# Attention in exact fp32 for all batches, and partition maxima on TensorE, in an attention and two-layer mixture-of-experts kernel

## The chip, the cores and the metric

The kernel runs on one core of a Trainium2 chip. A core has TensorE (in the profile PE for products, PEld for weight loads), VectorE (DVE), ScalarE (ACT), GpSimd (POOL) and SyncE (SP, which here starts the DMA transfers of inputs). The metric is the device time of one execution in microseconds; lower is better.

## The reference

Sparse attention of 4 batches, 8 heads, 576 positions and 64 dimensions; four heads see a local window of 32 positions, four every 32nd position. Its output is the input of a mixture of 8 experts with Sinkhorn-balanced gate, and that one's output the input of a second mixture, whose tokens are assigned greedily by sorted logits.

```python
def _attn_ref(q, k, v):
    scores = scale * np.matmul(q, k.transpose(0, 1, 3, 2))
    mask_local = (rel >= 0) & (rel < 32)
    mask_strided = (rel >= 0) & (pos[None, :] % 32 == pos[:, None] % 32)
    ...
    scores = scores - np.max(scores, axis=-1, keepdims=True)
    attn = np.exp(scores)
    attn = attn / (np.sum(attn, axis=-1, keepdims=True) + 1e-09)
    return np.matmul(attn, v)

def _moe_ref(x, w_gate, w1, w2):          # x: 2304 x 512
    P = np.exp(x @ w_gate - max)          # then 8 times: rows, columns to sum 1, times N / E
    for e in range(8):
        out += P[:, e:e + 1] * (np.maximum(x @ w1[e], 0.0) @ w2[e])

def _moe2_ref(x, w_gate, w1, w2):         # each token to one expert, 288 to each
    ...
```

## The kernel before

Large products are made in f16 with a split of each operand into a high and a low half: high by high, high by low and low by high, three f16 products in place of one fp32 product. Weights and inputs are scaled by a power of two, which needs the absolute maximum of the whole tensor, so a maximum over partitions: `att_scale` for V of each batch, `w_scale` for expert weights, `gate_w` for the gate. VectorE reduces along the columns, and `partition_all_reduce` on GpSimd over the 128 partitions (lines 194, 485, 546).

The attention works in units: batch, kind of mask (local with 6 groups of 96 queries by 128 keys; strided with 8 groups of 72 by 72) and pair of heads, 16 units, four to a batch. Within a unit the two heads lie on partitions 0 to 63 and 64 to 127 of q and k. The steps of a unit are load (L), halves of q and k (K, `att_k`, line 235), scores (S0, S1, `att_s`), mask and maximum (M), exponentials (E), row sums, reciprocal and normalising (N, the multiply on GpSimd, line 325), transposes of the probabilities by a product with the identity (T), and output products with V (O), whose result is split into the high and low half of x (`split_out`, lines 232 and 233). M, E, N and T are made for each head (0 or 1) by itself, O for each half of the groups.

Batch 0 (`EXACT`) is in plain fp32: one product per group and head, the mask added on TensorE by a bf16 product with the identity, the maximum read from PSUM, exponentials with the maximum as bias. Batches 1 to 3 use halves: q, k, the probabilities and V are split (V in `att_v`), the mask is added on VectorE (294), the maximum subtracted on GpSimd (297). While batch 0 is worked on, `busy` (158) puts extra bf16 products on TensorE, whose results are not used.

In the same stage run, by one string of letters (`SEQ`, line 47), the preparation of expert 0's weights (W for w1, V for w2: four column maxima, the scale, eight splits of 512 columns each), V of batch 1 (E), the load of w2 (R), the gate (G, H), constants (C), and Q: the first six jobs of 256 tokens of expert 0, as three pairs of jobs. A pair is 32 units: 16 groups of 12 products in layer 1 (`l1`, 614, with high half on ACT 617, low half on DVE 618) and 16 quarters of 24 products in layer 2 (`l2`, 632). A pair needs x of its tokens, so pair 1 batch 0, pair 2 batch 1, pair 3 batch 2. Each letter issues the next step of its generator; every engine works through its own instructions in the order in which they are issued, and waits where an operand or a buffer isn't ready. After the last letter the gate of the last five blocks of tokens (`gate(13, NT)`) ends the stage.

PSUM has eight banks: four with the tag "bank" (scores, transposes, outputs) and four "l1" (expert 0, gate, and batch 0's second kind of use).

The rest of the kernel, from the softmax of the gate on, is left as it is: expert 0's other jobs and experts 1 to 7, the second gate, the assignment, the second mixture.

Of the kernel before, what the change touches and what calls it, by code (L numbers as in the profile page):

```python
# [51 lines left out]
SPAD = 2  # L52
# [49 lines left out]
class Kernel:  # L102
# [11 lines left out]
    def abank(self, u, name):  # L114

        return self.bank(name, "l1" if u[0] == 0 and u[2] == 0 else "bank")
# [15 lines left out]

    def att_consts(self, pool):
# [3 lines left out]
        self.mk, self.mb = [], []  # L137
        for kind in range(2):
            P, G, W = self.GEO[kind]
            m = self.acc[:P, 16 + kind, 0:4 * W].rearrange("p (g w) -> p g w", w=W)  # L140
            nc.sync.dma_start(out=m, in_=self.a[f"mask{kind}"])
            self.mk.append(m)
# [5 lines left out]
        self.att_v_tiles(pool)  # L148

    GEO = (96, 6, 128), (72, 8, 72)  # L150
    GROUPS = ((0, 4), (4, 6)), ((0, 4), (4, 8))
    KQ = WIN + 2 * S
# [7 lines left out]
    def att_load_v(self, b, parts=None):  # L160

        nc = self.nc
        if not parts:
            parts = []
            for n, p, g in (("vl", 128, 6), ("vs", 72, 8)):
                t = self.ald.tile([p, 4, g, D], F32, name=n, bufs=1)
                nc.sync.dma_start(out=t, in_=self.a[n][b])
                parts.append((t[:, 0:2], t[:, 2:4]))
        else:
            for ts, n in zip(parts, ("vl", "vs")):  # L170
                for hp, t in enumerate(ts):
                    nc.sync.dma_start(out=t, in_=self.a[n][b, :, 2 * hp:2 * hp + 2])
        self.avr[b] = parts
# [7 lines left out]
    def att_scale(self, b):  # L181
# [3 lines left out]
        mx = sm.tile([128, 8], F32, name="vmx")  # L185
        nc.gpsimd.memset(mx, 0.0)
        for kind, p in enumerate((128, 72)):
            for hp, t in enumerate(self.avr[b][kind]):
                k = 2 * kind + hp
                nc.vector.tensor_reduce(mx[0:p, k:k + 1], t, axis=AX.XYZ, op=OP.max, apply_absolute_value=True)  # L190
                yield
        nc.vector.tensor_reduce(mx[:, 0:1], mx, axis=AX.X, op=OP.max)
# [16 lines left out]
    def att_v_tiles(self, pool):  # L209

        self.av = []
        for kind, (p, g) in enumerate(((128, 6), (72, 8))):
            ts = [pool.tile([p, 2, g, 192], F16, name=f"v{x}{kind}") for x in "ho"]
            for t in ts:
                self.nc.gpsimd.memset(t[:, :, :, D:2 * D], 0.0)
            self.av.append(ts)
# [256 lines left out]
    def w_scale(self, r, j, inv, early):  # L473
# [12 lines left out]
        if early:  # L486
            yield
# [999 lines left out]
```

## Time and profile before

| | |
|---|---|
| median of 3 runs | 2003.76 us (2003.56 to 2011.95) |
| the profiled execution | 2007.91 us |
| its span, first to last instruction | 2006.2 us, mean granted clock 0.969 |
| TensorE products, busy | 1889.4 us, 94% of the span |
| VectorE, ScalarE, GpSimd, busy | 1146.1, 526.4, 227.4 us |
| first product of expert 0 (line 614) | 81.45 us |
| last gate product of the stage (line 566) | ends at 306.64 us |

Times are those of one profiled execution. A busy TensorE is not one at its peak: products are pipelined, so in a dense row the time from start to start is the price, not the length. The granted clock is a share of full speed (2.4 GHz); 0.5 is the lower of its two levels, 1.2 GHz. A wait is put down to what came last before it ended.

### The profile page before, as it was taken

The numbers are of one execution on the slowest core, as the hardware profiler recorded it, in microseconds if no ns is written. First come the engines' busy times: TensorE is split into PE (matmuls) and PEld (weight loads), VectorE is DVE, ScalarE is ACT, GpSimd is POOL, SyncE is SP. The second block draws the span as 40 slices with busy tenths as digits, with TensorE's granted clock in tenths as the row PEclk, the third lists the DMA queues.
The fourth block names the chain that finished last, engine by engine and source line by source line (L and its number), as shares of the span: only waits on it lengthen the run. The fifth ranks groups of instructions, "written<-read, shape, count | busy, mean of one in ns | idle before, by whom it ended". The sixth has DMA issues, their size and how long they took to land. (4 is left out here: it accounts for less than half of the span.)

```text
span 2006.2 us, 29660 instructions
## 1 busy us (share of the span) xinstructions
PE 1889.4 (94%) x12406; PEld 1051.3 (52%) x12406; DVE 1146.1 (57%) x2779; ACT 526.4 (26%) x944; POOL 227.4 (11%) x250
## 2 busy tenths in 40 slices
PE   5579899999999999999999999999999999989997
PEld 3457576444544454445445444545454444666676
DVE  5677667465536554665455465434854788665530
ACT  3355343132122222111122123121201110232343
POOL 2426430000000000000000000000000003132231
PEclk7689999999999999999999999999999999999999
DMA  5302002114422431211134214321100003344360
GB/s 179 116 13 77 19 7 86 42 46 146 145 84 84 168 121 56 76 43 43 42 126 168 84 69 150 118 84 43 42 1 11 22 22 124 112 171 144 117 216 25
DMA packets 54302, 172.65 MB, mean 86 GB/s; under 512 B 4736, under 2 KB 9416, under 8 KB 49728
## 3 DMA queue, kind: packets, MB, share of 16 engines
q1 hardware_dynamic: 46488, 127.75, 18.0%
q0 software_dynamic: 7680, 43.01, 6.0%
q8 instruction: 97, 1.59, 0.3%
q14 instruction: 37, 0.30, 0.1%
HBM read 127.20 MB, written 43.54 MB: 85 GB/s over the span
## 5 line engine op out<-in xcount | busy, mean ns | idle before, releaser
L614 PE MATMUL l<-xh,w1h 128*128 128x512 f16 (+1 forms) x1408 | 482.8, 343 | 20.8 <-DVE hl L618 19.7
L614 PE MATMUL l<-xl,w1h 128*128 128x512 f16 (+1 forms) x1408 | 482.9, 343 | 0.0
L614 PE MATMUL l<-xh,w1l 128*128 128x512 f16 (+1 forms) x1408 | 482.6, 343 | 0.0
L632 PE MATMUL l<-w2h,hh 128*128 128x512 f16 x1152 | 438.3, 380 | 0.0
L632 PE MATMUL l<-w2h,hl 128*128 128x512 f16 x1152 | 438.0, 380 | 0.0
L632 PE MATMUL l<-w2l,hh 128*128 128x512 f16 x1152 | 437.9, 380 | 0.0
L614 PEld LDWEIGHTS <-w1h 128*128 128x128 f16 x2816 | 276.9, 99 | 249.6 <-issue 23.8
L617 ACT ACTIVATE hh<-l 128x512 f16<-128x512 f32 (+1 forms) x352 | 180.9, 517 | 767.5 <-PE l L614 767.1
L632 PEld LDWEIGHTS <-hh 128*128 128x128 f16 x2304 | 222.7, 98 | 260.4 <-issue 4.3
L618 DVE SCALAR_TENSOR_TENSOR hl<-l,hh 128x512 f16<-128x512 f32 (+1 forms) x352 | 206.2, 589 | 224.8 <-ACT hh L617 224.5
L664 DVE SCALAR_TENSOR_TENSOR acc<-l,pe,acc 128x512 f32<-128x512 f32 x126 | 94.2, 747 | 193.2 <-PE l L632 192.9
L614 PEld LDWEIGHTS <-w1l 128*128 128x128 f16 x1408 | 139.1, 99 | 112.9
L632 PEld LDWEIGHTS <-hl 128*128 128x128 f16 x1152 | 112.9, 98 | 136.8 <-issue 1.6
L479 DVE TENSOR_REDUCE wmx<-raw 128x1 f32<-128x1024 f32 x120 | 141.2, 1209 | 68.3 <-DMA raw<-in_moe_w_dram 68.3
L485 POOL PARTITION_ALL_REDUCE wall<-wmx x32 | 11.3, 352 | 974.5 <-DVE wmx L483 962.6
L498 ACT ACTIVATE m2h<-raw,wscale 128x1024 f16<-128x1024 f32 x64 | 70.4, 1140 | 192.1 <-DVE iw L492 89.0
L499 DVE SCALAR_TENSOR_TENSOR m2l<-raw,wscale,m2h 128x1024 f16<-128x1024 f32 x64 | 80.1, 1281 | 49.7 <-DMA wd<-m2l 28.4
L789 DVE SCALAR_TENSOR_TENSOR junk<-acc,raw 128x512 f32<-128x512 f32 x144 | 98.9, 687 | 3.3 <-DMA raw<-gt 1.4
L1258 DVE TENSOR_TENSOR h2l<-h,h2h 128x288 f16<-128x288 f32 x64 | 28.9, 454 | 65.4 <-ACT h2h L1257 58.2
L824 DVE SCALAR_TENSOR_TENSOR junk<-raw 128x256 f32<-128x256 f32 x128 | 54.1, 423 | 11.1 <-DMA raw<-in_moe_w_dram 7.6
L498 ACT ACTIVATE w2h<-raw,wscale 128x1024 f16<-128x1024 f32 x28 | 30.1, 1137 | 94.8 <-DVE wscale L129 94.8
L325 POOL TENSOR_TENSOR sm<-sm,den 96x768 f32<-96x768 f32 (+1 forms) x32 | 43.0, 1345 | 89.9 <-DVE den L323 26.5
(342 smaller groups left out, 1892.1 us busy)
## 6 DMA issues: line engine op xcount, KB each, us to landing
raw<-in_moe_w_dram SPq DMA_DIRECT2D x30, 2048.0 KB, 9.2
wd<-m2h SPq DMA_DIRECT2D x32, 512.0 KB, 2.6
wd<-m2l SPq DMA_DIRECT2D x32, 512.0 KB, 3.1
kq<-in_qk_dram SPq DMA_DIRECT2D x16, 592.0 KB, 3.8
acc<-in_moe_w_dram SPq DMA_DIRECT2D x2, 2048.0 KB, 10.9
vl<-in_vl_dram SPq DMA_DIRECT2D x3, 768.0 KB
raw<-gt SPq DMA_DIRECT2D x2, 1024.0 KB, 6.3
raw<-in_moe_w_dram SPq DMA_DIRECT2D x2, 1024.0 KB, 8.7
```

Of the source, the lines that this page charges most:

```text
L325: e.tensor_tensor(sm, sm, den[:, :, None].to_broadcast([P, G, W]), op=OP.mult)
L479: nc.vector.tensor_reduce(mx[:, k:k + 1], r[:, k * n:k * n + n], axis=AX.XY, op=OP.max, apply_absolute_value=True)
L498: nc.scalar.activation(hi, raw, AF.Copy, scale=s)
L499: nc.vector.scalar_tensor_tensor(lo, raw, s, hi, op0=OP.mult, op1=OP.subtract)
L614: nc.tensor.matmul(ps, l[:, d, fs], r[:, d, t0:t0 + nb], start=k == 0, stop=k == 3 * DC - 1)
L617: self.last = [nc.scalar.activation(hh[:, f, :nb], ps, AF.Relu).ins, nc.vector.scalar_tensor_tensor(hl[:, f, :nb], ps, 0.0, hh[:, f, :nb], ...
L618: nc.vector.scalar_tensor_tensor(hl[:, f, :nb], ps, 0.0, hh[:, f, :nb], op0=OP.max, op1=OP.subtract).ins]
L632: nc.tensor.matmul(ps, l[:, f, js], r[:, f], start=k == 0, stop=k == 3 * FC - 1)
L664: self.last = [nc.vector.scalar_tensor_tensor(a, ps, pe[:, c:c + 1], a, op0=OP.mult, op1=OP.add).ins]
L789: self.nc.vector.scalar_tensor_tensor(junk, self.acc[:, c], 1.0, self.wgb[:, e], op0=OP.mult, op1=OP.mult, accum_out=self.lg[:, c, e:e + 1])
L824: nc.vector.scalar_tensor_tensor(junk[:, :n], w[:, c], 1.0, g[:, e], op0=OP.mult, op1=OP.mult, accum_out=part[:, i, c, e:e + 1])
L1258: nc.vector.tensor_tensor(hl[:, f], r, hh[:, f], op=OP.subtract)
```

## The change

All four batches take the fp32 path. The step is now a piece: half the groups of a unit (3 of the local kind, 4 of the strided), both heads together in one instruction where an instruction can hold them, 32 pieces. The halves of q, k, probabilities and V go (`att_k`, `att_v`, `att_early`, `att_side`), and so do the mask on VectorE and the subtraction on GpSimd. Output products (O) and their split into x (X) are steps of their own. Scores have a pair of banks "s" (batch 0 alternates with "t"), transposes from batch 1 on a pair "t", outputs one bank "o", everything else three banks "l1".

The maxima over partitions in this stage (V of each batch, the gate's weights, both weights of expert 0) are made by `all_max`: a product with the identity brings the columns to rows, VectorE reduces them and puts the results on a diagonal, a product with ones spreads them to all partitions, and VectorE reduces again. The other experts' weights stay with GpSimd. w2's splits of expert 0 all go by ACT and DVE (`WM`), `busy` is called with 3, 5 and 1 products rather than 2 each, masks get buffers of their own, V has two buffers, and `SEQ` puts four Q to each piece from batch 1 on (`UNIT`).

```diff
--- before
+++ after
-EXACT = (0,)
-BUSY = 2, 2, 2, 2
+BUSY = 3, 5, 1
 START = 20
 PAD = 4
-PSCALE = 1024.0
 KQ_BUFS, SM_BUFS, P_BUFS = 3, 3, 2
-NORM = ("pp", "pp", "pp", "pp")
-PRO = "V V V V M0 M1", "E0", "N0", "E1", "N1 V V"
-FIRST = [("L K S0 S1", "M0", "E0", "T0", "T1", "M1", "E1", "N0", "O0", "N1", "O1")] * 4
-NEXT = "L K S0 S1 M0", "T0 M1", "T1", "E0 N0", "O0", "E1 N1", "O1"
-SIDE = 4
+PRO = "S0 M0", "S1 M1", "E0", "N0"
+FIRST = "S2 M2", "O-1", "E1", "X-1", "T0", "N1"
+TURN = "S1 M1", "O-1", "E1", "X-1", "T0", "N1"
+NEXT = "S1 M1", "O-1", "E1", "X-1", "T0", "N1"
+UNIT = "AQAAQAQQAA"
+SEQ = ("A" * 12 + "AWAWAWAW" + "R" + "A" * 4 + "WAWAWA" + "AWAWAWAWAWAWAWAW" + "A" * 11 + "AVAAVAAVAAVAAAAA" + "VAQVAAVQVAQVQAAV" + "VAQAAVQVAQVQAAV" + "VVU" + "UUUUUAAA" +
+       "G" + "U" * 8 + "AAHC" + "U" * 8 + "AA").replace("U", UNIT) + "Q" * 20
+WM = "aaaaaaaa"
+SPAD = 0
 NW = 8
-UNIT = "AQQAQAQAQAQAQAQ"
-UNIT = "AQQAQAQAQAQAQAQ"
-LESS = "AQQAQAAQAAQA"
-UNIT = "AQQAQAQAQAQAQAQ"
-LESS = "AQQAQAAQAAQA"
-SEQ = ("A" * 12 + "AWAWAWAW" + "R" + "A" * 6 + "W" + "AWAWAWAWAWAWAWAWAWAW" + "A" * 10 + "AVAVAVAV" + "AAAEE" + "A" + "EQ" * 4 + "VEQ" * 2 + "A" + "VEQVEQ" + "AEVQAVQ" + "EVQEVQ" + "EVQ" + "EVEVQA" + "AEVQLLL" +
-       "GUUUUHCUUUU").replace("U", UNIT).replace("L", LESS) + "Q" * 20
-WM = "aaaapapa"
-EPAD = 1
-VPAD = 0
-SPAD = 2
...
+    def all_max(self, cols, out):
+        nc = self.nc
+        k = cols.shape[1]
+        yield
+        ps = self.bank("amx", "l1")
+        nc.tensor.matmul(ps[:k, 0:128], cols, self.identf, start=True, stop=True)
+        m = self.asm.tile([4, 1], F32, name="amax")[:k]
+        nc.vector.tensor_reduce(m, ps[:k, 0:128], axis=AX.X, op=OP.max)
+        d = self.asm.tile([4, 4], F32, name="adiag")[:k, :k]
+        nc.vector.tensor_scalar(d, self.identf[:k, :k], m, None, op0=OP.mult)
+        yield
+        yield
+        nc.tensor.matmul(ps[:, 128:128 + k], self.onesf[:k], d, start=True, stop=True)
+        nc.vector.tensor_reduce(out, ps[:, 128:128 + k], axis=AX.X, op=OP.max)
...
+    GROUPS = ((0, 3), (3, 6)), ((0, 4), (4, 8))
-    GROUPS = ((0, 4), (4, 6)), ((0, 4), (4, 8))
...
-        nc.gpsimd.partition_all_reduce(al, mx[:, 0:1], channels=128, reduce_op=bass_isa.ReduceOp.max)
-        yield
+        yield from self.all_max(mx, al)
...
-    def att_v_tiles(self, pool):
-    def att_v(self, b, kind):
-    def att_k(self, u):
...
+    def piece(self, k):
+        u = self.us[k // 2]
+        P, G, W = self.GEO[u[1]]
+        g0, g1 = self.GROUPS[u[1]][k % 2]
+        return u, P, W, g0, g1 - g0
+    def wide(self, tag, name):
+        return self.psum.tile([128, 2, 512], F32, name=name, tag=tag, bufs=1)
+    def att_s(self, k):
+        nc = self.nc
+        (b, kind, hp), P, W, g0, n = self.piece(k)
+        G = self.GEO[kind][1]
+        kq = self.aqk[b, kind, hp]
+        ps = self.aps[k] = self.wide("t" if b == 0 and k % 2 else "s", "ps")
+        m = self.mb[kind][:, min(k % 2, 1 - kind):][:, 0:n].rearrange("p g w -> p (g w)")
+        for j in range(2):
+            if b == 0:
+                self.busy(ps[:, j], BUSY[0])
+            nc.tensor.matmul(ps[:P, j, :n * W], self.identb[:P, :P], m, start=True, stop=False)
+        for g in range(n):
+            kc = slice((g0 + g) * P, (g0 + g) * P + W)
+            qc = slice(pad + (G + g0 + g) * P, pad + (G + g0 + g + 1) * P)
+            for j in range(2):
+                pj = slice(64 * j, 64 * j + 64)
+                nc.tensor.matmul(ps[:P, j, g * W:(g + 1) * W], kq[pj, qc], kq[pj, kc], start=False, stop=g == n - 1)
+    def scores(self, k):
+        u, P, W, g0, n = self.piece(k)
+        return self.aps[k][:P, :, :n * W].rearrange("p j (g w) -> p j g w", w=W)
+    def att_m(self, k):
+        nc = self.nc
+        u, P, W, g0, n = self.piece(k)
+        mx = self.asm.tile([96, 2, 4], F32, name="mx")[:P, :, :n]
+        nc.vector.tensor_reduce(mx, self.scores(k), axis=AX.X, op=OP.max)
+        nc.vector.tensor_scalar(mx, mx, -1.0 / math.sqrt(D), None, op0=OP.mult)
+        self.amx[k] = mx
+    def att_e(self, k):
+        nc = self.nc
+        u, P, W, g0, n = self.piece(k)
+        ps, mx = self.scores(k), self.amx.pop(k)
+        sm = self.aw.tile([96, 1024], F32, name="sm", bufs=SM_BUFS)[:P, :2 * n * W]
+        sm = self.asc[k] = sm.rearrange("p (j g w) -> p j g w", j=2, w=W)
+        for j in range(2):
+            for g in range(n):
+                nc.scalar.activation(sm[:, j, g], ps[:, j, g], AF.Exp, bias=mx[:, j, g:g + 1], scale=1.0 / math.sqrt(D))
+    def att_n(self, k):
+        nc = self.nc
+        u, P, W, g0, n = self.piece(k)
+        sm = self.asc[k]
+        den = self.asm.tile([96, 2, 4], F32, name="den")[:P, :, :n]
+        nc.vector.tensor_scalar(den, den, 1e-9, None, op0=OP.add)
+        nc.gpsimd.tensor_tensor(sm, sm, den[:, :, :, None].to_broadcast([P, 2, n, W]), op=OP.mult)
+    def att_t(self, k):
+        nc = self.nc
+        u, P, W, g0, n = self.piece(k)
+        sm = self.asc.pop(k)
+        t = self.aw.tile([128, 2, 288], F32, name="p", bufs=P_BUFS)[:W, :, :n * P]
+        self.apf[k] = t.rearrange("p j (g w) -> p j g w", w=P)
+        early = u[0] == 0
+        pt = None if early else self.wide("t", "ptp")
+        for j in range(2):
+            ps = self.bank("ptp", "l1") if early else pt[:, j]
+            if early:
+                self.busy(ps, BUSY[1])
+            for g in range(n):
+                nc.tensor.transpose(ps[:W, g * P:(g + 1) * P], sm[:, j, g], self.identf[:P, :P])
+            if early:
+                nc.scalar.activation(t[:, j], ps[:W, :n * P], AF.Copy)
+        if not early:
+            nc.scalar.activation(t, pt[:W, :, :n * P], AF.Copy)
+    def att_o(self, k):
+        nc = self.nc
+        (b, kind, hp), P, W, g0, n = self.piece(k)
+        po = self.apo[k] = self.bank("po", "o")
+        pf = self.apf.pop(k)
+        if b == 0:
+            self.busy(po, BUSY[2])
+        for g in range(n):
+            for j in range(2):
+                nc.tensor.matmul(po[64 * j:64 * j + 64, g * P:(g + 1) * P], self.avr[b][kind][:, 2 * hp + j, g0 + g],
+                                 pf[:, j, g], start=True, stop=True)
+    def att_x(self, k):
+        (b, kind, hp), P, W, g0, n = self.piece(k)
+        src = self.apo.pop(k)[:, :n * P]
+            hi, lo = (x[:, dc, t0 + g0 * P:t0 + (g0 + n) * P] for x in (self.xh, self.xl))
+            hi, lo = (x[:, dc, t0:t0 + S].rearrange("p (m j) -> p m j", j=8)[:, :, g0:g0 + n] for x in (self.xh, self.xl))
+        self.split_out(hi, lo, src, self.avs[b][:, 0:1])
+        self.avr, self.avs, self.aqk, self.asc, self.amx, self.apf, self.aps, self.apo = ({} for _ in range(8))
+        self.us = [(b, kind, hp) for b in range(B) for kind in range(2) for hp in range(2)]
+        last = 2 * len(self.us)
+        fs = {"S": self.att_s, "M": self.att_m, "E": self.att_e, "N": self.att_n, "T": self.att_t, "O": self.att_o,
+              "X": self.att_x}
+        def load(k):
+            if k < len(self.us):
+                self.att_load(self.us[k])
+        def run(k, text):
+                i = k + int(w[1:])
+                if 0 <= i < last and (w[1:] != "-1" or k % 8):
+                    fs[w[0]](i)
+        load(0)
+        load(1)
+        yield
+            run(0, w)
+        side = self.att_scale(0)
+        for k in range(last):
+            if k % 2 == 0:
+                load(k // 2 + 2)
+            if k == 4 or k in (8, 16):
+                self.att_load_v(k // 8 + 1)
+            if k in (8, 12, 20):
+                side = self.att_scale((k + 7) // 8)
+            if k == 10:
+                side = self.gate_w(self.sm, self.graw)
+            for w in (FIRST if k < 6 else TURN if k < 8 else NEXT) + ("O0", "X0") * (k % 8 == 7):
+                run(k, w)
                 next(side, None)
                 yield
-    def att_side(self, b):
-    def att_early(self):
...
-        nc.gpsimd.partition_all_reduce(al, m2, channels=128, reduce_op=bass_isa.ReduceOp.max)
         if early:
-            yield
+            yield from self.all_max(mx, al)
+        else:
+            nc.gpsimd.partition_all_reduce(al, m2, channels=128, reduce_op=bass_isa.ReduceOp.max)
...
-        nc.gpsimd.partition_all_reduce(al, mx, channels=128, reduce_op=bass_isa.ReduceOp.max)
-        yield
+        yield from self.all_max(mx, al)
...
-        self.banks = {"bank": 4, "l1": 4}
+        self.banks = {"l1": 3, "o": 1}
...
-            gens = {"A": att, "W": self.w_prep(0, w0, (r1, r2), (0,)), "E": self.att_early(), "R": late(raw2),
+            gens = {"A": att, "W": self.w_prep(0, w0, (r1, r2), (0,)), "R": late(raw2),
```

## Rows read from the trace of the kernel before

**Rows 1.** Windows by stage: length, busy us (count) per engine, TensorE clock, DMA.
```profile
0.00:81.45 81.45, 51.12 (x454) 37.28 (x455) 53.94 (x111) 32.85 (x95) 27.32 (x31) 0.70 0.51 167
81.45:152.00 70.55, 43.67 (x411) 32.62 (x409) 41.99 (x96) 27.40 (x57) 19.14 (x19) 0.79 0.09 26
152.00:217.00 65.00, 55.06 (x748) 42.47 (x747) 46.15 (x104) 29.30 (x61) 32.99 (x23) 0.95 0.19 60
217.00:306.70 89.70, 87.47 (x1024) 60.72 (x1022) 56.80 (x132) 38.61 (x83) 39.07 (x35) 1.00 0.09 30
306.70:2006.20 1699.50, 1652.06 (x9774) 878.26 (x9774) 947.19 (x2338) 398.23 (x650) 108.91 (x144) 0.99 0.25 89
```

**Rows 2.** TensorE's waits, 0 to 307 us: waiting line, releaser, total, times, longest.
```profile
PE ps L272 <- DVE xl L233: 21.8, 8, 7.1
PE l L614 <- DVE hl L618: 15.0, 2, 12.3
...
PE ptp L344 <- POOL sm L325: 6.8, 2, 3.6
```

**Rows 3.** Timeline of GpSimd: start, length, instruction, idle time before and its releaser.
```profile
29.80 0.38 POOL L194 PARTITION_ALL_REDUCE vall<-vmx  x1 [5.74 <-issue]
37.81 1.46 POOL L325 TENSOR_TENSOR sm<-sm,den 96x768 f32<-96x768 f32 x1 [7.63 <-ACT xh L232]
...
210.02 0.38 POOL L194 PARTITION_ALL_REDUCE vall<-vmx  x1 [5.71 <-issue]
217.41 1.14 POOL L325 TENSOR_TENSOR sm<-sm,den 72x576 f32<-72x576 f32 x1 [7.02 <-ACT hh L617]
```

**Rows 4.** Timeline of TensorE: expert 0's products at full clock, first and last.
```profile
84.63 0.27 PE L614 MATMUL l<-xh,w1h 128*128 128x256 f16 x1
...
88.12 0.27 PE L614 MATMUL l<-xh,w1l 128*128 128x256 f16 x1
...
163.21 0.38 PE L632 MATMUL l<-w2l,hh 128*128 128x512 f16 x1
...
165.37 0.38 PE L632 MATMUL l<-w2h,hl 128*128 128x512 f16 x1
```

**Rows 5.** Windows of line 566 (gate) alone: TensorE and weight loads, clock, DMA.
```profile
81.45:217.00 135.55, 2.86 (x108) 2.80 (x108) 0.87 0.14 42
```

**Rows 6.** Timeline of TensorE: attention products, fp32 (batch 0), last one f16.
```profile
16.07 0.68 PE L272 MATMUL ps<-kq 64*96 64x128 f32 x8
...
34.33 1.62 PE L367 MATMUL po<-p,vl 128*64 128x96 f32 x16
...
41.53 0.74 PE L272 MATMUL ps<-kq 64*72 64x72 f32 x16
...
42.44 0.50 PE L344 MATMUL ptp<-identf,sm 96*128 96x96 f32 x4
...
175.17 1.21 PE L272 MATMUL ps<-kq 64*96 64x128 f16 x36
```

**Rows 7.** Groups by line and shape, 0 to 307 us: busy, mean ns, idle before.
```profile
L618 DVE SCALAR_TENSOR_TENSOR hl<-l,hh 128x256 f16<-128x256 f32 x48 | 19.6, 410 | 7.7 <-ACT hh L617 7.7
L321 DVE TENSOR_REDUCE den<-sm 96x6 f32<-96x768 f32 x16 | 15.1, 941 | 3.4 <-ACT sm L312 2.0 <-ACT sm L310 1.4
...
L479 DVE TENSOR_REDUCE wmx<-acc 128x1 f32<-128x1024 f32 x8 | 9.4, 1197 | 0.0
...
L322 DVE TENSOR_SCALAR den<-den 96x6 f32<-96x6 f32 x16 | 3.0, 189 | 0.6
...
L291 DVE TENSOR_REDUCE mx<-ps 96x4 f32<-96x512 f32 x4 | 2.7, 678 | 0.0
...
L233 DVE SCALAR_TENSOR_TENSOR xl<-po,vscale,xh 128x288 f16<-128x288 f32 x4 | 2.0, 489 | 0.0
...
L310 ACT ACTIVATE sm<-ps,mx 96x128 f32<-96x128 f32 x24 | 6.5, 382 | 11.1 <-DVE mx L292 11.0
...
L325 POOL TENSOR_TENSOR sm<-sm,den 96x768 f32<-96x768 f32 x16 | 24.1, 1508 | 45.4 <-DVE den L323 14.3 <-ACT sm L310 13.9 <-ACT xh L232 9.7
```

**Rows 8.** Line 499 by itself (w1's low halves): count, duration min/median/max, first, last.
```profile
L499 DVE SCALAR_TENSOR_TENSOR w1l<-acc,wscale,w1h x8: 698/742/4726, 50.7 to 63.3; 128x512 f16<-128x512 f32 x8
```

More of the change, by code (lines that the diff above doesn't have):

```diff
@@ L158, in busy, with att_load_v @@
             self.nc.tensor.matmul(ps[:, 0:256], w[:, 0:128], w, start=True, stop=True)
[L160 to L172, printed above, removed]
+    def att_load_v(self, b):
+        parts = []
+        for n, p, g in (("vl", 128, 6), ("vs", 72, 8)):
+            t = self.ald.tile([p, 4, g, D], F32, name=n)
+            self.nc.sync.dma_start(out=t, in_=self.a[n][b])
+            parts.append(t)
         self.avr[b] = parts
@@ L207, in att_scale @@
         yield
-    def att_v_tiles(self, pool):
[L211 to L216, printed above, removed]
-    def att_v(self, b, kind):
-        nc = self.nc
-        p = (128, 72)[kind]
-        raw = self.avr[b][kind]
-        s = self.avs[b][0:p, 0:1]
-        for h in range(4):
-            hi, lo = (t[:, h // 2, :, 128 * (h % 2):128 * (h % 2) + D] for t in self.av[kind])
-            v = raw[h // 2][:, h % 2]
-            nc.scalar.activation(hi, v, AF.Copy, scale=s)
-            nc.vector.scalar_tensor_tensor(lo, v, s, hi, op0=OP.mult, op1=OP.subtract)
-            yield
     def split_out(self, hi, lo, src, s=1.0):
@@ L275, in scores @@
-    def scores(self, u, j, half):
-        P, G, W = self.GEO[u[1]]
-        g0, g1 = self.GROUPS[u[1]][half]
-        return self.aps[u][j][half][:P, :(g1 - g0) * W].rearrange("p (g w) -> p g w", w=W)
-    def att_m(self, u, j):
-        nc = self.nc
-        b, kind, hp = u
-        P, G, W = self.GEO[kind]
-        mx = self.asm.tile([P, G], F32, name=f"mx{kind}")
-        sm = self.aw.tile([96, 768], F32, name="sm", bufs=SM_BUFS)[:P, :G * W].rearrange("p (g w) -> p g w", w=W)
-        self.asc[u, j] = sm, mx
-        for half, (g0, g1) in enumerate(self.GROUPS[kind]):
-            ps = self.scores(u, j, half)
-            if b in EXACT:
-                nc.vector.tensor_reduce(mx[:, g0:g1], ps, axis=AX.X, op=OP.max)
-                nc.vector.tensor_scalar(mx[:, g0:g1], mx[:, g0:g1], -1.0 / math.sqrt(D), None, op0=OP.mult)
-            else:
-                nc.vector.tensor_tensor(sm[:, g0:g1], ps, self.mk[kind][:, min(half, 1 - kind):][:, 0:g1 - g0], op=OP.add)
-        if b not in EXACT:
-            nc.vector.tensor_reduce(mx, sm, axis=AX.X, op=OP.max, negate=True)
-            nc.gpsimd.tensor_tensor(sm, sm, mx[:, :, None].to_broadcast([P, G, W]), op=OP.add)
@@ L299, in att_e @@
-    def att_e(self, u, j):
-        nc = self.nc
-        b, kind, hp = u
-        P, G, W = self.GEO[kind]
-        sm, mx = self.asc[u, j]
-        sc = 1.0 / math.sqrt(D)
-        if b in EXACT:
-            for half, (g0, g1) in enumerate(self.GROUPS[kind]):
-                ps = self.scores(u, j, half)
-                for g in range(g0, g1):
-                    nc.scalar.activation(sm[:, g], ps[:, g - g0], AF.Exp, bias=mx[:, g:g + 1], scale=sc)
-        else:
-            nc.scalar.activation(sm, sm, AF.Exp, scale=sc)
@@ L314, in att_n @@
-    def att_n(self, u, j):
-        nc = self.nc
-        b, kind, hp = u
-        P, G, W = self.GEO[kind]
-        sm, _ = self.asc[u, j]
-        den = self.asm.tile([P, G], F32, name=f"den{kind}")
-        nc.vector.tensor_reduce(den, sm, axis=AX.X, op=OP.add)
-        nc.vector.tensor_scalar(den, den, 1e-9, 1.0 if b in EXACT else 1.0 / PSCALE, op0=OP.add, op1=OP.mult)
-        nc.vector.reciprocal(den, den)
-        e = nc.vector if NORM[b][j] == "v" else nc.gpsimd
-        e.tensor_tensor(sm, sm, den[:, :, None].to_broadcast([P, G, W]), op=OP.mult)
@@ L356, in att_o @@
         dc = 2 * kind + hp
         t0 = b * S
-        g0, g1 = self.GROUPS[kind][half]
-        po = self.abank(u, "po")
-        if b in EXACT:
-            self.busy(po, BUSY[2])
-        for g in range(g0, g1):
-            o = po[:, (g - g0) * P:(g - g0 + 1) * P]
-            if b in EXACT:
-                v = self.avr[b][kind]
-                for j in range(2):
-                    nc.tensor.matmul(o[64 * j:64 * j + 64], v[hp][:, j, g], self.apf[u, j][0][:, g],
-                                     start=True, stop=True)
-            else:
-                vh, vo = (t[:, hp, g] for t in self.av[kind])
-                k = 0
-                for j in range(2):
-                    ph, pl = self.apf[u, j]
-                    js = slice(64 * j, 64 * j + 128)
-                    for l, r in ((vh, ph), (vo, ph), (vh, pl)):
-                        nc.tensor.matmul(o, l[:, js], r[:, g], start=k == 0, stop=k == 5)
-                        k += 1
```

144 lines of the change are left out of this document (15 added, 129 removed).

## Prediction

> **What bounds the kernel now.** I read the windows by stage first: they say which stretch can give anything. From 306.7 us to the end TensorE is busy for 1652 of 1699.5 us, and the change touches nothing there, so that part moves as a block. The first 306.7 us hold the whole attention, the preparation of the first expert's weights, the gate and the first 1536 tokens of expert 0; there TensorE is busy 237 us, at a granted clock of 0.70, 0.79, 0.95 and 1.00 of full in four stretches [rows 1]. No other engine is full: VectorE 54 of 81, 42 of 71, 46 of 65, 57 of 90 us. So the stage is bound by waiting until about 217 us, and by TensorE only in the last 90 us (87.5 busy). What is looked for is the end of the stage, 306.7 us.
>
> Second view, what TensorE waits for in that stage [rows 2]: scores for a bank that the output's eviction must free (21.8 us in 8 waits), expert 0's products for an eviction (15.0, one of 12.3), transposes for a multiply of GpSimd (6.8). The first two name ACT and VectorE, which are not busy, so I followed the waits to GpSimd, third view. A maximum over partitions there comes after 5.7 us of waiting on nothing but issue, and the next ordinary multiply 7 to 8 us after it [rows 3] (the first and the last of six such pairs, one of which holds two maxima; they end at 38, 56, 98, 113, 152 and 217 us). Each takes GpSimd away for about 13 us, 78 us in all. Normalising the probabilities needs GpSimd, so the attention stands still behind it, and VectorE and TensorE behind the attention: the long waits of [rows 2] lie inside these six stretches.
>
> The Trainium skill (GPSIMD Engine Reference, section on the path of an instruction to execution) puts about 6 us on the first call of freshly loaded code. By that alone a maximum would cost 6 us, the six 36 us; the rows also show the way back, and the measurement decides.
>
> **The change, part by part.** All seven maxima leave GpSimd in this stage, and with them the 78 us; also its subtraction of the maximum, its low halves of q and k, and four w2 pieces. What stays on it is one multiply for each of 32 pieces, 1.5 us for the larger kind [rows 7].
>
> Cost of one attention piece (half a unit, both heads), by prices of the exact batch 0 at full clock. TensorE: a local piece has 6 score products (8 in 0.68 us: 0.4), 6 transposes (4 in 0.50 us with the tail: 0.5), 6 output products (16 in 1.62 us, but at half clock, so 0.6 there and an estimated 0.3 at full) and two mask products (estimated 0.3); a strided one 8 score products (16 in 0.74 us: 0.35) and the like [rows 6]. I take 1.46 us for either. VectorE: maximum 0.95 (0.678 for 512 columns, scaled to 768), row sums 0.94, low half 0.49, three small ones of 0.19: 2.9 us local, 2.5 strided by fewer columns, mean 2.7 [rows 7]. ScalarE: 6 exponentials of 0.27, high half and copy about 0.6 each: 2.8 us. Each is under the TensorE time of a piece with its filling, below.
>
> The f16 form that goes away costs 36 score products in 1.21 us, 0.034 each and three for one fp32 product of 0.042 to 0.076 [rows 6]: TensorE work falls or stays. The Trainium skill (FP8 and Floating Point Precision, TensorE Precision Notes) says true fp32 takes four passes through the array, which speaks against the change: four against three. It is rival 2.
>
> First stretch, until expert 0's first product (81.45 us now). VectorE's queue decides it after the first loads: its work is 8 pieces (22 us), one more maximum since the schedule names piece 7's scores twice and one for piece 8 (2), V's four maxima (some 4.3), w1's and w2's eight maxima at 1.2 (9.6) and eight low halves of w1 at 0.74 (5.9) [rows 7, 8], small ones 2: 46 us, against 54 now [rows 1]. The first maximum no longer stands behind V's, which wait for their load, and can begin near 9 us; table load and first exponentials bring the loop's start to about 13 us. 13 + 46 minus what is done by then (2), plus 5 for the last piece's transpose, copy, product and eviction one after another, is 62; TensorE at half clock gives 4 more (a piece's 17 or 18 busy products of 256 columns, 142 in all against 80 now, at twice the 0.109 of [rows 4] are 3.7 us, with twice 1.46 it is 6.6, where VectorE has only 2.5 to 4): **66 us**, bounds 59 and 78. On SP's queue w1's load now stands before the third and fourth kq load, and w2's raw load no longer behind a kq load that waits for its buffer; masks have a place of their own. All this lands before it is used; if not, it costs the maxima's wait, a few us, inside the bounds.
>
> Then 24 pieces, with four units of expert 0 behind each, exactly 32 units to a batch. TensorE's work at full clock: layer 1 has 12 products of 0.109 us in a unit (33 starts in 3.49 us), layer 2 24 of 0.216 in four units (11 starts in 2.16 us) [rows 4], so 1.3 us a unit, 96 units 124.8 us; 24 pieces 35.0; the gate 216 products, 108 in 2.86 us [rows 5], 5.5. Sum **165 us**. A piece takes 5.2 + 1.46 = 6.7 us, in which VectorE has 2.7 + four evictions of 0.41 = 4.4 [rows 7] and ScalarE as much. The exceptions:
> - Pieces 8 and 9 also carry w2's eight low halves (now all on VectorE, with ACT's high halves), V's next maxima and two row-to-column maxima: VectorE 21 us against 13.4 of TensorE. **+7** (0 to 14, if GpSimd's multiply slows the low halves as in the 4.7 us maximum of [rows 8]).
> - After batches 1, 2 and 3 the last output product and its eviction stand with nothing beside them, and the gate behind: copy, product, two evictions, about 2 us each. **+6** (0 to 9).
> - Scores have one pair of banks and transposes another: scores of the next piece wait in TensorE's queue for this piece's exponentials, and expert 0, output product and transposes stand behind them. By the times above the exponentials end some 2 us earlier than that. Expert 0 has three banks instead of four-and-shared. The maximum over partitions adds two waits of TensorE on VectorE, seven times (batch 0's and w1's lie in the first stretch); behind them the next scores; their small products cost 0.1 us each. For all of these and a spell of half clock **+6** (0 to 25; the trace has no row for them; nearest are the last 90 us, where an order written the same way loses 2.2 us, and the 65 before with one stall of 7).
>
> End of the stage: 66 + 165 + 7 + 6 + 6 = **250 us**, against 306.7: 56.5 us less. The next maximum on GpSimd, of the softmax over experts, has its code loaded while the last piece runs, as now. Profiled: span 2006.2 - 56.5 = 1949.7, with the 1.7 us around it 1951.4. The profiled execution is 4.15 us over the median of the three runs, so the median comes to **1947 us**.
>
> **Rivals.**
> 1. GpSimd was only one of several late things, and VectorE or ScalarE takes its place: each piece at 7.5 to 8 us rather than 6.7, first stretch at 74. For it: VectorE's four kinds of work in one strict order, 60 to 71% busy already [rows 1]. Against: its sum falls by more than the pieces add. 74 + 165 + 19 + 24 x 0.8 = 277: 1974 us.
> 2. fp32 products of batches 1 to 3 cost four thirds of the three f16 ones, 0.136 for 0.034 x 3, so 0.09 us more than the 0.05 taken, on some 14 products of a piece and 24 pieces: 30 us. End 280, 1977 us. That is what the page's four passes make of it. Against: every fp32 row of batch 0.
> 3. Slower than before: the single pairs of banks put a piece's whole chain on TensorE's queue: scores 0.8, maximum 1.1, exponentials 1.7, sums and reciprocal 1.3, multiply 1.5, transposes 0.5, copy 0.65, with hand-overs 8.3 us, and no unit of expert 0 beside it. It decides once a piece takes over 9.9 us: (317 - 66 - 12) / 24. In full it is 8.3 + 5.2 = 13.5 us a piece, 24 x 6.8 = 163 us more: 2110 us. For it: the 21.8 us of bank waits of [rows 2]. Against: scores are issued a whole piece ahead, transposes a whole piece after their multiply, and output banks are now apart.
> 4. The gain is there but given back after 306.7 us, by weights of expert 1 or a table that now come late. Its price is at most the gain itself, so 2004 us; TensorE's 97% there leaves little room for it.
>
> **How the numbers follow.** Forecast 68%, its own range 1929 to 1966; rival 1 17%; rival 2 4%; rival 3 8%, of which 6 beyond its deciding point and 2 short of it near no change; rival 4 3%. The range reaches from the low bounds (59 + 165 + 9 = 233, 1930) to rivals 1 and 2 with the upper bounds of stalls: 1929 to 1984; some 5% lie below and 13% above. About 0.5% (10 us) is what a measurement of this kernel tells from no change: faster 0.89, same 0.05, slower 0.06.
>
> **What would show it.** GpSimd without any maximum over partitions before the stage's end and no wait on issue of over 5 us; first product of expert 0 near 66 us; the gate's last product near 250 us; TensorE over 90% busy and at 1.00 clock from batch 2 on; fp32 scores at 0.04 to 0.08 us each. Wrong would be: a wait of scores on exponentials of over a us in most pieces (rival 3), VectorE over 85% busy from 70 to 250 us (rival 1), or more TensorE idle time than now behind 250 us (rival 4).

## The result, and the profile after

| | before | after |
|---|---|---|
| median | 2003.66 us (4 runs, 2000.40 to 2011.95) | 1971.45 us (4 runs, 1967.03 to 1977.06) |
| profiled execution, span | 2007.91, 2006.2 us | 1974.22, 1972.5 us |
| first product of expert 0 | 81.45 us | 73.35 us |
| end of the stage (gate's last product) | 306.64 us | 274.23 us |
| from there to the end of the span | 1699.6 us | 1698.3 us |

The changed kernel takes 0.983 of the time before (95% interval 0.980 to 0.986): 32 us less, where 56.5 were forecast. All of it lies in the stage (306.6 to 274.2).

The changed kernel's windows, cut at the first product of expert 0 and at the gate's three bursts (columns as in [rows 1]: length, then busy us and count of PE, PEld, DVE, ACT, POOL, then clock, DMA share, GB/s):

```profile
0.00:73.35 73.35, 54.58 (x492) 40.01 (x493) 46.42 (x91) 30.16 (x95) 14.12 (x20) 0.82 0.51 173
73.35:146.38 73.03, 66.78 (x603) 44.84 (x601) 48.33 (x111) 34.37 (x101) 10.81 (x9) 0.97 0.16 51
146.38:212.69 66.31, 65.40 (x698) 46.71 (x696) 35.90 (x77) 29.29 (x92) 11.91 (x19) 0.97 0.14 46
212.69:274.23 61.54, 60.90 (x666) 44.03 (x664) 28.52 (x71) 27.55 (x86) 9.03 (x8) 1.00 0.09 23
274.23:1972.50 1698.27, 1650.44 (x9774) 877.50 (x9774) 945.75 (x2338) 397.92 (x650) 108.52 (x144) 0.99 0.25 89
```

From batch 2 on TensorE is 99% busy; before it was 85% from 152 to 217 us and 98% from there to the stage's end [rows 1]. GpSimd's 33 and 39 us have become 12 and 9. What is left of TensorE's waits, 0 to 275 us (columns as in [rows 2]):

```profile
PE ptp L286 <- POOL sm L270: 7.6, 3, 2.8
PE amx L113 <- DVE vmx L185: 5.1, 3, 3.0
PE ps L158 <- ACT sm L259: 2.7, 2, 1.5
PE amx L113 <- DVE gmx L450: 2.4, 1, 2.4
```

The wait of 21.8 us of [rows 2] is gone, and of the 15.0 us 1.1 are left. Of TensorE's idle time, 26.6 us, 18.8 lie in the first 73 us. What the maximum by products adds is small: 5.1 us in three waits for V, one of them (3.0) in the first stretch, and 2.4 for the gate.

### The profile page after: what moved, and what is told of

Its sections match the earlier page's. It is cut to its first block, busy times and chain, and to the rows that moved or that the text cites. A ratio compares the mean times of both kernels' runs of the same rounds, so it can differ in the third digit from the quotient of the medians.

```text
span 1972.5 us, 29232 instructions
## 1 busy us (share of the span) xinstructions
PE 1898.1 (96%) x12226; PEld 1053.1 (53%) x12226; DVE 1104.9 (56%) x2688; ACT 519.3 (26%) x1024; POOL 154.4 (8%) x199
## 4 chain that ended last, share of the span: by engine, by line
PE 70%; DVE 15%; DMA 7%; issue 3%; ACT 2%; another core or an unknown queue 1%; POOL 1%; SPq 0%; POOLq 0%; DVEq 0%; ACTq 0%
PE l L537 28%; PE l L519 28%; DMA raw<-in_moe_w_dram 6%; DVE wmx L384 4%; PE mm L1186 3%; PE mm L1156 3%; DVE hl L523 2%; DVE m2l L405 2%; DVE w2l L405 2%; DVE w1l L405 1%; PE pcnt L825 1%; PE ps L235 1%; PE po L302 1%; DMA wd<-m2l 1%
## 5 line engine op out<-in xcount | busy, mean ns | idle before, releaser
L259 ACT ACTIVATE sm<-ps,mx 72x72 f32<-72x72 f32 (+1 forms) x224 | 54.4, 339 | 37.7 <-DVE mx L247 29.6
```

Source lines behind the costliest of these rows:

```text
L259: nc.scalar.activation(sm[:, j, g], ps[:, j, g], AF.Exp, bias=mx[:, j, g:g + 1], scale=1.0 / math.sqrt(D))
```

## The experiments

Median, ratio to the runs of the kernel before beside it, with its interval, and the marks of the profiled execution:

| | us | ratio | first product | stage end | rest of span |
|---|---|---|---|---|---|
| changed kernel | 1971.5 | 0.983 (0.980 to 0.986) | 73.35 | 274.23 | 1698.3 |
| the same again (e8) | 1973.2 | 0.984 (0.979 to 0.989) | 72.71 | 273.58 | 1692.7 |
| pieces alone, maxima on GpSimd (e1) | 1997.8 | 0.995 (0.994 to 0.997) | 82.34 | 299.77 | 1696.6 |
| maxima alone (e2) | 1984.1 | 0.988 (0.986 to 0.990) | 83.92 | 292.14 | 1692.8 |
| scores made twice (e3) | 1991.5 | 0.992 (0.990 to 0.994) | 69.78 | 290.91 | 1699.4 |
| 16-bit products (e4) | 1959.5 | 0.977 (0.974 to 0.980) | 68.34 | 260.66 | 1698.5 |
| no unused products (e5) | 1968.8 | 0.981 (0.979 to 0.983) | 68.01 | 268.73 | 1698.9 |
| twice the unused products (e6) | 1966.2 | 0.981 (0.976 to 0.985) | 69.79 | 269.32 | 1694.8 |
| trimmed (e7) | 1960.5 | 0.977 (0.973 to 0.982) | 65.51 | 263.18 | 1691.7 |
| trimmed, again (e10) | 1956.9 | 0.975 (0.973 to 0.978) | 65.66 | 262.32 | 1689.4 |
| trimmed, preparation moved (e9) | 1957.7 | 0.976 (0.973 to 0.978) | 64.52 | 261.21 | 1690.1 |

The rest of the span is the same code in all of them, and differs by 10 us, two executions of the changed kernel by 5.6. Most of that lies at the kernel's end and goes with the granted clock: the same last part took 332 us (before) and 329 (changed) at 0.94, 325 (e8) and 324 (e10) at 0.96. So the marks of the stage, each of one profiled execution, say more than the medians.

### The maxima and the pieces, each alone

The changed kernel with the seven maxima back on GpSimd:

```diff
-        nc.tensor.matmul(ps[:k, 0:128], cols, self.identf, start=True, stop=True)
-        nc.vector.tensor_reduce(m, ps[:k, 0:128], axis=AX.X, op=OP.max)
...
+        nc.vector.tensor_reduce(m, cols, axis=AX.X, op=OP.max)
+        nc.gpsimd.partition_all_reduce(out, m, channels=128, reduce_op=bass_isa.ReduceOp.max)
```

> The changed kernel with its seven early maxima over partitions back on GpSimd (line 113 on), everything else as changed. Theory A, the gain is the removal of these maxima: each takes GpSimd away for some 13 us and normalising stands behind it, so the stage ends 30 to 65 us later than 274 us (305 to 340) and the time is 2000 to 2037 us. Theory B, the gain is the fp32 pieces with both heads, and maxima are hidden beside other work: under 1985 us.

And the kernel before with `all_max` in place of its maxima, at its three call sites:

```diff
-        nc.gpsimd.partition_all_reduce(al, mx[:, 0:1], channels=128, reduce_op=bass_isa.ReduceOp.max)
-        yield
+        yield from self.all_max(mx, al)
```

> The kernel before, with f16 halves and its own order, and only the seven early maxima made by small products on TensorE. Theory A: most or all of the gain, 1960 to 1980 us; the long waits of TensorE (7.1 for scores, 12.3 for expert 0) go, what is late next is the order of the first pair of jobs. Theory B: above 1995 us.

Measured by the medians: pieces alone gain 0.5% (9 us), maxima alone 1.2% (23 us), both together 1.7%. Both results lie between what the two theories expected, and neither part is the whole gain. By the marks the two parts do not simply add up: the stage ends 6.9 us earlier with the pieces alone, 14.5 with the maxima alone, 32.4 with both. Behind expert 0's first product they do (225.2 us become 217.4, 208.2 and, with both, 200.9). The first stretch gains only when both are changed (81.45 us become 82.3, 83.9 and 73.35). TensorE's waits, 0 to the stage's end, show what is missing to the full gain. The first line is of the kernel with the pieces alone, where transposes wait on GpSimd's multiply; the second is of the one with the maxima alone, where 9.6 us are left of the 21.8 of [rows 2]:

```profile
PE ptp L280 <- POOL sm L264: 24.4, 8, 8.4
PE ps L284 <- DVE xl L245: 9.6, 6, 6.0
```

Expert 0's wait of 15.0 us is gone with the maxima alone, but there the maxima's own small products wait 22.9 us for their operands: the old order of work isn't made for them, so 14.5 us is what they bring in it and not all that GpSimd's standstill cost. GpSimd's timeline in the kernel with the pieces alone, two maxima and the multiply behind each:

```profile
103.83 0.38 POOL L113 PARTITION_ALL_REDUCE vall<-amax  x1 [5.79 <-issue]
111.72 1.46 POOL L264 TENSOR_TENSOR sm<-sm,den 96x768 f32<-96x768 f32 x1 [7.51 <-DVE gmx L444]
118.99 0.38 POOL L113 PARTITION_ALL_REDUCE gall<-amax  x1 [5.80 <-issue]
126.23 1.46 POOL L264 TENSOR_TENSOR sm<-sm,den 96x768 f32<-96x768 f32 x1 [6.87 <-DVE hl L517]
```

The pair of 5.8 and 7 us of [rows 3] is there again under quite another schedule, so it belongs to the maximum and not to the old order of work. The 78 us that the six stretches took from GpSimd are worth 14.5 us at the stage's end under the old order of work and 25.5 under the new one (299.77 against 274.23); the rest was hidden behind other work.

### The price of a product

Scores and mask of batches 1 to 3 made twice, the second time over the first:

```diff
-        for j in range(2):
+        for again in range(1 if b == 0 else 2):
+            for j in range(2):
...
```

> The changed kernel, where the mask and score products of batches 1 to 3 are made twice into the same banks. Added work of TensorE by the changed kernel's rows: mask 3.1 and scores 6.0 us a batch, 27 us in all. Theory C, TensorE bounds the pieces from batch 1 on: 22 to 28 us more than the changed kernel, 1992 to 2000 us. Theory D, a product's price lies beside waits: under 12 us more.

And scores and outputs of these batches from the upper 16 bits of each operand, read as bf16, in one pass:

```diff
+                kl = kq if b == 0 else kq.bitcast(BF16).rearrange("p (c t) -> p c t", t=2)[:, :, 1]
+                nc.tensor.matmul(ps[:P, j, g * W:(g + 1) * W], kl[pj, qc], kl[pj, kc], start=False, stop=g == n - 1)
...
+                if b:
+                    l, r = (x.bitcast(BF16).rearrange("p (c t) -> p c t", t=2)[:, :, 1] for x in (l, r))
```

> The changed kernel, where scores and output products of batches 1 to 3 read only the upper 16 bits of each fp32 number as bf16, so that a product is one instruction in place of two; this leaves out the low bits of q, k, V and the probabilities. Theory C, the forecast was late by the price of fp32 products (two instructions of 0.05 us each, taken as one) and TensorE bounds the pieces: 24 pieces x 14 products x some 0.06 us = 20 us less, the stage ends near 254 us and the time is 1946 to 1956 us. Theory D, waits between the engines bound the pieces and the price of a product is hidden: less than 7 us gained, above 1964 us.

Windows of batch 2 with one line alone (PE, PEld): the scores and the outputs of the changed kernel, then the scores and the outputs in 16 bits:

```profile
146.38:212.69 66.31, 6.55 (x114) 5.13 (x112) 0.97 0.14 46
146.38:212.69 66.31, 5.75 (x112) 4.40 (x112) 0.97 0.14 46
```

```profile
137.48:202.79 65.31, 2.82 (x60) 1.76 (x56) 0.92 0.16 48
137.48:202.79 65.31, 2.62 (x56) 1.60 (x56) 0.92 0.16 48
```

A batch has 56 score products and 56 output products (4 pieces of 6 and 4 of 8). In fp32 each stands as two instructions, 112; in 16 bits as one, 56 (a few records more are parts of a split group). That is the key to the miss: rows of fp32 products count half products. From start to start 112 score instructions take 6.0 us and 112 output instructions 5.3, so 0.107 and 0.095 us a product; the 16-bit ones 2.3 and 2.1 us, 0.040 and 0.038.

These are means of two shapes, and part of batch 2 is at half clock. In unbroken groups at full clock, from the first start to the next group's, an fp32 product costs 0.138 us in local scores, 0.084 in strided ones, 0.108 and 0.082 in local and strided outputs. In 16 bits these four cost 0.051, 0.033, 0.043 and 0.032, so fp32 is 2.5 to 2.7 times as dear. Three f16 products of the kernel before cost 0.095, 0.060, 0.128 and 0.098. One strided group of scores from there (48 instructions for 16 products), then groups of the changed kernel (8 products in each strided row, 6 in the local one):

```profile
275.53 1.03 PE L272 MATMUL ps<-kq 64*72 64x72 f16 x48
```

```profile
188.03 0.74 PE L235 MATMUL ps<-kq 64*72 64x72 f32 x16
188.70 0.72 PE L302 MATMUL po<-p,vs 72*64 72x72 f32 x16
203.49 0.90 PE L235 MATMUL ps<-kq 64*96 64x128 f32 x12
```

What the price is worth in time, TensorE's windows of the last two stretches, with scores twice and then in 16 bits:

```profile
148.33:222.65 74.32, 74.32 (x827) 53.03 (x825) 35.70 (x77) 29.14 (x92) 11.96 (x19) 0.98 0.12 38
222.65:290.91 68.26, 67.62 (x766) 48.71 (x764) 28.10 (x71) 27.61 (x86) 8.98 (x7) 1.00 0.09 21
```

```profile
137.48:202.79 65.31, 62.05 (x589) 41.37 (x585) 35.69 (x77) 29.11 (x92) 10.69 (x11) 0.92 0.16 48
202.79:260.66 57.87, 55.94 (x568) 38.64 (x564) 29.32 (x72) 27.30 (x87) 10.26 (x16) 1.00 0.10 26
```

From the first product of expert 0 to the stage's end the changed kernel takes 200.9 us. Some 25 us more work (mask 9, scores 16) makes it 221.1, +20; the median is 18 to 20 us up, just under theory C's 22 to 28 and far from D. Some 19.5 us less (scores 10, outputs 9.5) makes it only 192.3, -8.6: TensorE then idles 13.4 us in place of 7.8, and its other products cost 5 us more, the granted clock being 0.92 in batch 2 of this execution. The median gained 12 us, between theories C and D. So dearer products are paid at four fifths, cheaper ones return under half. TensorE is the bound, with little room below it.

### The first stretch

Unused products taken away, and doubled:

```diff
-BUSY = 3, 5, 1
+BUSY = 0, 0, 0
```

> The changed kernel without its 142 unused products in batch 0. Theory E, TensorE's queue at half clock makes the first stretch longer than forecast: first product of expert 0 at 62 to 69 us in place of 73.4, time 4 to 11 us less. Theory F, the chain from VectorE over GpSimd to the transposes decides there and the unused products only keep the clock up: first product at 72 to 80 us, time the same or up to 7 us more.

```diff
-BUSY = 3, 5, 1
+BUSY = 6, 10, 2
```

> The changed kernel with its unused products of batch 0 doubled (284 in place of 142, 22 us more of TensorE). Theory E, TensorE's queue lies on the path of the first stretch: first product of expert 0 at 80 to 95 us, time 7 to 20 us more. Theory F, VectorE and GpSimd decide there: first product by 76 us, time within 3 us.

The first product of expert 0 came at 68.0 us with none, at 73.4 and 72.7 with 142, at 69.8 with 284: that doubling costs 7 us or more has fallen. Without them theory E's mark held (62 to 69 us), and the time fell by 3 to 4 us, about the least of the 4 to 11 that it expected; with twice as many, theory F's mark held, and the time is 5 to 7 us under the changed kernel's, where 3 either way were expected. The same 142 stand in the kernels with scores twice and in 16 bits, with the mark at 69.8 and 68.3 and a mean clock of 0.89 and 0.88, where the changed kernel has 0.82 and 0.84. Score groups of the first batch, in TensorE's timeline, of the changed kernel, then with none, then with twice as many (two groups each, at about the same point of the work):

```profile
20.44 1.60 PE L235 MATMUL ps<-kq 64*96 64x128 f32 x12
26.38 0.74 PE L235 MATMUL ps<-kq 64*72 64x72 f32 x16
```

```profile
20.94 1.60 PE L235 MATMUL ps<-kq 64*96 64x128 f32 x12
25.77 1.24 PE L235 MATMUL ps<-kq 64*72 64x72 f32 x16
```

```profile
22.25 0.90 PE L235 MATMUL ps<-kq 64*96 64x128 f32 x12
28.71 0.74 PE L235 MATMUL ps<-kq 64*72 64x72 f32 x16
```

The same 12 instructions take 1.60 us at half clock and 0.90 at full. Without unused products all rows of the stretch have the lengths of half clock, with 284 those of full clock from 8 us on, with 142 they alternate. The mean clock of a window misleads here: it counts the time before the first step that the trace holds as full (the first 10 us of the changed kernel, 28 us without unused products), though the first score group takes 1.60 us in every one of these runs. What they win in clock they take in time: the chain that ends with expert 0's first product holds 9 us of them in the changed kernel. A part of that chain (start, length, what):

```profile
46.54 1.46 POOL sm L270
48.04 0.70 PE ptp L286 x4
48.74 1.07 PE ptp L158 x5
49.80 0.48 PE ptp L286 x4
50.28 0.64 PE ps L158 x3
50.92 0.24 PE ps L229
51.16 0.64 PE ps L158 x3
```

Line 158 is the unused products; the transposes (286) and the masks (229) wait behind them on TensorE.

Then a kernel with four trims: no unused products, piece 7's scores once, two of w2's low halves back on GpSimd and the gate's weights four pieces later. The changed kernel stood beside it once more:

```diff
-BUSY = 3, 5, 1
+BUSY = 0, 0, 0
-TURN = "S1 M1", "O-1", "E1", "X-1", "T0", "N1"
+TURN = "", "O-1", "E1", "X-1", "T0", "N1"
-WM = "aaaaaaaa"
+WM = "aaaapapa"
-            if k == 10:
+            if k == 14:
-            for w in (FIRST if k < 6 else TURN if k < 8 else NEXT) + ("O0", "X0") * (k % 8 == 7):
+            for w in (FIRST if k < 6 else TURN if k < 7 else NEXT) + ("O0", "X0") * (k % 8 == 7):
```

> The changed kernel without unused products, without the second making of piece 7's scores, with every second quarter of w2's split on GpSimd as before, and the gate's maximum moved from piece 10 to piece 14. Theory E, the first stretch is held by TensorE's queue, and batch 1 by VectorE's: first product of expert 0 at 62 to 68 us, batch 1 some 3 to 6 us shorter, 6 to 14 us less than the changed kernel. Theory F, the first stretch is held by VectorE and GpSimd: within 5 us of the changed kernel.

> The changed kernel unchanged, beside the others on one chip. The kernel with one-instruction products began expert 0 at 68.3 us and the changed one at 73.4, though they are alike up to there. Theory G, this difference is the phase of the clock's steps: the first product lies between 66 and 76 us again, not at 73.4, and the time is 1963 to 1980 us. Theory H, it belongs to the kernel: 73 to 74 us again.

The trimmed kernel is the better one: 12.6 us under the changed kernel beside it, with the first product 7 us earlier, the stage's end 10, and batch 1 in 69.8 us rather than 73.0, all as theory E had it. What each trim gave by itself wasn't measured, but for the unused products. Its first stretch is at half clock from one end to the other and still the shorter: the score group at 64 us takes 1.60 us as the first does, and the trace's first step of the clock is at 66.7 us, where expert 0's products fall from 0.42 to 0.27 us.

The changed kernel's second execution began expert 0 at 72.7 us. That lies in theory G's range and a third of a us short of H's, so it doesn't tell them apart. What goes with the difference is the clock. Windows of the changed kernel, of its second execution, of the kernel with scores twice and of the one in 16 bits, whose edits come into play only behind them:

```profile
47.50:56.50 9.00, 8.46 (x65) 6.57 (x66) 6.02 (x14) 4.37 (x17) 1.63 (x2) 0.50 0.01 2
47.50:56.50 9.00, 9.00 (x68) 6.92 (x69) 5.76 (x13) 4.11 (x14) 1.24 (x2) 0.50 0.01 2
47.50:56.50 9.00, 8.50 (x122) 6.92 (x120) 7.18 (x15) 4.84 (x19) 2.29 (x2) 1.00 0.15 45
47.50:56.50 9.00, 8.21 (x116) 6.65 (x117) 7.41 (x17) 4.90 (x17) 2.53 (x3) 1.00 0.03 4
```

Both executions of the one kernel spend these 9 us at half clock, the other two at full. That the 3 to 5 us between their first products are due to this is argued from it, and whether chance or the kernel puts the spell there stays open.

Last, in the trimmed kernel, the weight preparation moved behind the row sums in VectorE's order (only the letters up to the first Q):

```diff
-SEQ = ("A" * 12 + "AWAWAWAW" + "R" + "A" * 4 + "WAWAWA" + "AWAWAWAWAWAWAWAW" + "A" * 11 + "AVAAVAAVAAVAAAAA" +
+SEQ = ("A" * 10 + "WWR" + "A" * 6 + "WWW" + "AW" + "A" * 5 + "WWW" + "A" * 6 + "WWW" + "A" * 6 + "WWW" + "A" * 6 + "VV" + "A" * 6 + "VV" + "A" * 8 +
```

> The trimmed kernel (e7) with one change: in the first stretch the letters W and V, which issue the maxima and splits of expert 0's weights on VectorE, stand behind the step that normalises a piece, three at a time, and no longer one after each step of the attention. The work is the same. Theory F: the first stretch is decided by VectorE's order. Row sums stand behind a weight maximum of 1.2 us or a split of 0.74 us, GpSimd's multiply behind the row sums, the transposes behind the multiply: with the order changed the three waits of transposes on GpSimd (7.6 us in the changed kernel) fall to under 3 us, the first product of expert 0 comes at 57 to 63 us in place of 65.5, and the time is 3 to 8 us under the trimmed kernel's on the same chip (about 1953 to 1958 us). Rival: the loads, or TensorE at half clock, decide the first stretch: first product at 64.5 us or later, time within 2 us of the trimmed kernel's.

> The trimmed kernel (e7) unchanged, on the same chip as the run with the moved preparation, to give the spread between executions: first product of expert 0 at 65 to 70 us, end of the stage at 262 to 266 us, 1958 to 1963 us. If it differs from its first run by more than the moved preparation differs from it, that comparison says nothing.

TensorE's waits up to the first product of expert 0, order of the letters as it was, then moved:

```profile
PE ptp L286 <- POOL sm L270: 7.9, 4, 3.7
PE ps L229 <- POOL mb L149: 4.1, 1, 4.1
PE amx L113 <- DVE vmx L185: 3.4, 1, 3.4
```

```profile
PE ps L229 <- POOL mb L149: 4.1, 1, 4.1
PE amx L113 <- DVE wmx L384: 4.0, 1, 4.0
PE amx L113 <- DVE vmx L185: 3.4, 1, 3.4
PE ptp L286 <- POOL sm L270: 3.0, 3, 1.2
```

The transposes' wait falls from 7.9 to 3.0 us as expected, and the first product comes only 1.1 us earlier; TensorE's idle time up to there is 22.9 us after 23.2. The medians are 0.8 us apart, less than the 3.6 between the trimmed kernel's two runs, so they say nothing; the trimmed kernel's first products differ by 0.15 us. The theory has fallen: the order moved the waits and shortened next to nothing. The rival's numbers held (64.5 us, within 2 us), but not its cause as written, since most of the chain of the moved kernel runs over VectorE; a stretch of it:

```profile
40.74 2.83 DVE w1l L405 x3
43.58 0.68 DVE mx L246
44.45 0.42 DVE xl L205
44.87 0.67 DVE den L267
45.96 2.84 DVE w1l L405 x3
48.80 0.68 DVE mx L246
```

So the chain points to VectorE's 46 us of work rather than to its order. No run shows it, and none has this stretch without unused products at full clock.

## Why the prediction was right or wrong

**Right: what bounded the kernel.** The waits on ACT and VectorE in [rows 2] were for the most part GpSimd's: with the maxima alone moved, the 15.0 us are gone and the 21.8 are 9.6. With the maxima alone moved, 1.2% is gained, with the pieces alone 0.5%; the first stretch needed both. Nothing came in their place: no wait of TensorE over 3.0 us is left in the stage. The Trainium skill's 6 us for the first call of freshly loaded code (GPSIMD Engine Reference, Instruction dispatch) is half of the pair; the way back to the ordinary multiply, 7 to 8 us, is in the rows alone. That GpSimd loads code in either half no run shows.

**Right: TensorE bound from batch 2 on, the end unmoved.** Busy 65.4 of 66.3 and 60.9 of 61.5 us; the rest of the span changed by 1.3 us. Rival 4 (given back later) didn't come. Rival 3 (a piece's chain on TensorE's queue) didn't either: no wait of scores on exponentials from batch 1 on stands in the waits.

**Wrong: the time, 1947 us against 1971.** The stage ended at 274.2 us in place of 250, 24 us later. That 1971 still lies in the whole range (to 1984) is owed to the room left there for rivals 1 and 2, not to the forecast. The terms, each from the sum of the starts in the three stretches:

| term | forecast | measured | difference |
|---|---|---|---|
| first product of expert 0 | 66 | 73.4 | +7.4 |
| 24 pieces on TensorE | 35.0 | 53.1 | +18.1 |
| expert 0's units | 124.8 | 130.7 | +5.9 |
| gate | 5.5 | 5.9 | +0.4 |
| exceptions (7, 6 and 6) | 19 | 11.1 | -7.9 |

- The failed step is the price of a piece, 1.46 us. Scores and outputs were taken from [rows 6] as if a row of x8 held eight products; it holds four. So a piece has 12 or 16 score instructions, 0.75 us on the mean and not 0.4, and outputs 0.66 and not 0.3. With masks of 0.39 and transposes of 0.50 that is 2.30 us in batch 2. The count could have been made: by GROUPS, in the diff, a local unit was issued in parts of four and of two groups, with two heads 8 and 4 products, and the x8 of [rows 6] is the part of two.
- Rival 2 had the direction of this, and for the local scores the price: 0.138 us an fp32 product at full clock, where three f16 ones cost 0.095 (its own numbers were 0.136 and 0.102). Strided scores cost 0.084 in place of 0.060. Output products went the other way, 0.108 in place of 0.128 and 0.082 in place of 0.098. Over a batch that makes 11.2 us in place of 10.4 (scores 6.0 in place of 4.2, outputs 5.2 in place of 6.2). So scores and outputs together cost neither about half of the f16 form, as the forecast's price had it, nor four thirds, and rival 2's 30 us were too many. The Trainium skill (FP8 and Floating Point Precision, TensorE Precision Notes) has four passes; beside the 16-bit product of the same shape the fp32 one costs 2.5 to 2.7 times as much here. How many passes that is the runs don't show.
- The units cost 1.36 us rather than 1.30: layer 1's products are 0.125 and 0.118 us apart in batches 1 and 2, where the granted clock is 0.97, and 0.109 in batch 3, where it is 1.00. The 0.109 of [rows 4] was a row at full clock.
- The exceptions were over-priced, which hid a part of the miss: 3.3 us of small products for the maxima and 7.8 us of idle time are all there is. Rival 1 (VectorE or ScalarE takes over) is refuted for the pieces: VectorE is 66% busy in batch 1 and 54% in batch 2.
- The first stretch lay inside its bounds (59 to 78) but not by its working. VectorE's 46 us of work is exact (46.4). The unused products, priced at 3.7 us, hold 9 us of the chain: without them the mark comes at 68.0, and with the other trims at 65.5. Without its 3.7 us the forecast would have been 62, so the rest of its working was short too, by nearly 6 us, and what holds these isn't shown. With 142 unused products nearly the same code gives 68.3 to 73.4, later where more of it is at half clock.

With products at the forecast's price the time would not have been 1947 either: 19.5 us less work brought 8.6 us; 5.6 us went to more idle time of TensorE and 5 to dearer products at a lower granted clock.

**Open:** why the granted clock at the kernel's end differs between executions (the unchanged rest of the span takes 1689 to 1700 us), and whether the first stretch can go under 64 us with less work on VectorE, which wasn't tried.

## What to carry to other kernels

An engine that stands still before a rare instruction and again behind it is found by following waits to the third engine. Its price is the time on both sides (13 us a maximum here), of which the kernel pays only what nothing covers (2 to 4 us for each of the six stretches). Before a row of the trace becomes a price, count its instructions against the loops of the code: a factor of two stood in plain sight. A sum of TensorE work is a bound only as long as nothing else waits beneath it; price a saving by what is late next, and a cost at nearly its full size (four fifths here).

## What the runs showed of the hardware

- One fp32 product on TensorE stands in the trace as two instructions, together 0.08 us (72 columns) to 0.14 us (128 columns) at full clock, 2.5 to 2.7 times a 16-bit product of the same shape. Three f16 products, which it replaced, took 0.095 and 0.060 us in scores, less than it, and 0.128 and 0.098 in outputs, more than its 0.108 and 0.082.
- GpSimd stood still on both sides of a maximum over partitions in both schedules: 5.7 to 6.0 us before most of them, and 7 to 8 us before the ordinary instruction after most of them (up to 7.7 and 9.6 with the pieces).
- Products that keep the clock up have a price that can equal their gain: none of them gave half clock and 68.0 us to expert 0's first product, 284 gave full clock from 8 us on and 69.8, 142 gave an alternating clock and 68.3 to 73.4.
